# A two-stage kernel (cross-covariance attention, then a sigmoid-gated feed-forward): one activation table set, norms by Newton roots, and one PSUM bank per tile pair

## The chip, the cores and the metric

The kernel runs on one core of a Trainium2 chip. The metric is the time of one execution on the device in microseconds (us), as the median of several runs. A core has five engines that run side by side and wait for each other by semaphores: PE (TensorE, matrix products into PSUM), DVE (VectorE), ACT (ScalarE), POOL (GpSimd) and SP (which here only issues transfers). Each engine takes its instructions strictly in its own order.

## What is computed

For each of 4 batches, q, k and v are 6016 x 256. The attention is over channels: a 256 x 256 score from the columns of k and q, each divided by its norm, a softmax, and v times that matrix. Its result goes through a gated feed-forward layer of width 1536:

```python
qn = q / (np.linalg.norm(q, axis=1, keepdims=True) + 1e-06)
kn = k / (np.linalg.norm(k, axis=1, keepdims=True) + 1e-06)
s = kn.transpose(0, 2, 1) @ qn / tau
a = np.exp(s - s.max(-1, keepdims=True))
a /= a.sum(-1, keepdims=True) + 1e-09
x = (v @ a).reshape(B * N, C)
gate = 1.0 / (1.0 + np.exp(-(x @ w_gate)))
out = gate * (x @ w_val) @ w_out
```

The output has 24064 rows of 256 numbers in fp32; tau is 1.

## The kernel before

**The algebra.** Since x = v a, the kernel multiplies a into the weights once per batch: G = a w_gate and H = a w_val (tiles `gh_G`, `gh_H`, 256 x 1536 each), so that gate and value come from v directly. The last product, with `w_out`, is done with seven products in place of eight (Strassen and Winograd's way, 128 x 128 blocks): from two row tiles (a *pair*) and two column blocks of `w_out`, five sums of `hT` blocks (`sums`, made by DVE, L501) and five sums of `w_out` blocks (`w_sums`, made once by POOL, L198) give seven products, each of six matmuls with 128 columns, 42 for a pair.

**Order of the work.** The order is written out by hand and nothing reorders it. A batch has 47 row tiles of 128, in 12 *chunks* of four tiles (the last has three). A chunk has 12 *steps*, f = 0 to 11, one for each 128 columns of the inner width. In each step `glu` (L462 on) issues two matmuls into `ps_gate`, two into `ps_val` (two PSUM buffers each), a sigmoid on ACT (L483, `g_sb`) and a multiply on DVE (L484, `hT`). Behind it, `run_work` (L592) issues its share of the matmuls of the chunk before, about seven a step, into `ps_o` (a pool of two PSUM banks). `a_sum` puts one of DVE's ten sums in each of the steps 0, 1, 3, 4, 5 and 7 to 11.

**The products' banks.** `PRODUCTS` (L33) splits a pair's seven products over two banks, four in the first, three in the second, each copied to SBUF by ACT (L564, 512 and 384 columns). A chunk of two pairs so wants four banks one after the other, of two that there are. The copies are put off: `flush(1)` issues one of them behind the next step's sigmoid. From the copies POOL builds the four output blocks with four additions of 256 columns (`combine`, L524 to L528), and SP stores the chunk (L610, at f = 6).

**Beside it, for the next batch** (`side_work`, L702): POOL issues the loads of q, k and v, PE accumulates the score in PSUM in chunks 0 to 7, ACT squares q and k (L233) and DVE adds the squares (L271); these are folded (L281 to L289, one piece every three steps from chunk 8 on) and summed by PE into `ps_n` at step 9 of chunk 9, for k in all 256 columns of every partition.

**At a batch's end** ACT needs Sqrt (`wide_sqrt`, L306) and Exp (`exps`, L380), which lie in other table sets than Sigmoid, so that four ACT_TABLE_LOADs come in at the ends of the chunks 9 and 10. There the kernel keeps three sevenths of the products back (`keep`) and runs them as a block of matmuls behind the last step, and lets the products of the next chunk begin two steps late (`late`). Between them DVE inverts the roots in two parts (`wide_inv`, L311 and L312, 128 or 130 columns) and scales the score (L322). In chunk 11 twelve `gh` fills (two matmuls of 512 columns, L411 on, then a scaled copy to SBUF on ACT L431 or DVE L433) make G and H of the next batch, two of them in the last step.

Batch 0's attention runs ahead of the loop (to 41.6 us), with a root by ACT and its own table loads.

Of the kernel before, what the change touches and what calls it, by code (L numbers as in the profile page):

```python
# [10 lines left out]
BF16 = mybir.dt.bfloat16  # L11
ACT = mybir.ActivationFunctionType
# [20 lines left out]
PRODUCTS = (  # L33
    ((1, 1), 0),
    ((0, 0), 1),
    (0, 2),
    (1, 3),
    (2, (1, 1)),
    (3, (0, 0)),
    (4, 4),  # L40
)
FIRST_BANK = 4
NEXT_SLOTS = (0, 1, 3, 4, 5)
OWN_SLOTS = (7, 8, 9, 10, 11)
# [3 lines left out]
def kernel(  # L48
# [20 lines left out]
    nc = tc.nc  # L69
# [30 lines left out]
    f32pool = pool("f32pool", 2)  # L100
# [191 lines left out]
    def norms_mm(b):  # L292

        s = st[b]
        fold_q, fold_k = s["fold"]
        ps = psm.tile([P, CB + C], FP32, tag="m", name="ps_n")
        norm_mms(ps, (fold_q,), 2, True, True, (0,))
        for u in range(2):
            mm(ps[:, CB:], ones_bf, fold_k[:, u, :], False, u == 1, skip_group_check=True)
        s["n"] = ps  # L300

    def wide_sqrt(b):
        s = st[b]
        s["n_sb"] = attp.tile([P, CB + C], FP32, tag="nsb", name="n_sb")
        s["r"], s["rk"] = s["n_sb"][:, :CB], s["n_sb"][:, CB:]
        nc.scalar.activation(out=s["n_sb"], in_=s["n"], func=ACT.Sqrt)  # L306

    def wide_inv(b, part):

        r = st[b]["n_sb"][:, (0 if part == 0 else CB + C // 2) : CB + (part + 1) * (C // 2)]  # L310
        nc.vector.tensor_scalar(out=r, in0=r, scalar1=1e-6, scalar2=None, op0=ALU.add)  # L311
        nc.vector.reciprocal(r, r)  # L312
        if part == 0 and inv_tau != 1.0:
            nc.vector.tensor_scalar(
                out=r[:, :CB], in0=r[:, :CB], scalar1=inv_tau, scalar2=None, op0=ALU.mult
            )

    def wide_scale(b):
        s = st[b]
        s["x"] = attp.tile([P, CB, C], FP32, tag="x", name="x_sb")  # L320
        for j in range(CB):
            nc.vector.scalar_tensor_tensor(  # L322
                out=s["x"][:, j, :],
                in0=s["s"][:, j, :],
                scalar=s["r"][:, j : j + 1],
                in1=s["rk"],
                op0=ALU.mult,
                op1=ALU.mult,
            )
# [56 lines left out]
    def sums_both(b):  # L386
# [14 lines left out]
        s["rrow"] = [r[:, i : i + 1] for i in range(CB)]  # L401
# [23 lines left out]
    def gh_store(b, n, ps, act):  # L425
# [3 lines left out]
        r = s["rrow"][i]  # L429
# [32 lines left out]
    def glu(b, ci, f, between=None):  # L462
# [8 lines left out]
        for ps, w in ((ps_gate, G), (ps_val, H)):  # L471
# [11 lines left out]
        nc.scalar.activation(out=g_sb[:, :n], in_=ps_gate[:, :n], func=ACT.Sigmoid)  # L483
        nc.vector.tensor_tensor(  # L484
            out=hts[b, ci][:, f, :n], in0=ps_val[:, :n], in1=g_sb[:, :n], op=ALU.mult
# [4 lines left out]
    def a_sum(b, ci, g, m):  # L490
# [4 lines left out]
        if m == 0:  # L495
# [13 lines left out]
    pending = []  # L509
# [20 lines left out]
    def out_work(b, ci):  # L530
# [310 lines left out]
```

## Time and profile before

| | |
|---|---|
| median of 3 runs | 853.62 us (853.47 to 854.08) |
| the profiled execution | 854.03 us; its span, first to last instruction, 852.2 us |
| granted TensorE clock, mean | 0.998 |
| busy, of the span: PE / DVE / ACT / POOL | 94% / 86% / 62% / 48% |
| chain of work that ended last: PE / DVE / ACT | 70% / 12% / 7% |
| sigmoid L483, 128x512 | 528 of 598 ns |
| multiply L484, 128x512 | 528 of 684 ns |
| sums L501, 128x768 | 440 of 627 ns |
| table loads: L306 / L796 / before the loop | 3 / 9 / 3, 1283 ns each |

A page of the profile gives each engine's busy time, the chain of waits that leads to the last instruction, and groups of like instructions with the idle time of the engine ahead of them and what ended it. A row of the timeline is start, length, engine, line, operation, output<-input and count, with the wait before it in brackets. A row of the windows gives a stretch and its length, then busy time and count of PE, PEld (weight loads), DVE, ACT and POOL, then clock and DMA. PE's times are modelled and overlap: a matmul's row is longer than its distance to the next one, so distances are read from start to start.

### The profile page before, as it was taken

The numbers are of one execution on the slowest core, as the hardware profiler recorded it, in microseconds if no ns is written. First come the engines' busy times: TensorE is split into PE (matmuls) and PEld (weight loads), VectorE is DVE, ScalarE is ACT, GpSimd is POOL, SyncE is SP. The second block draws the span as 40 slices with busy tenths as digits, with TensorE's granted clock in tenths as the row PEclk, the third lists the DMA queues.
The fourth block names the chain that finished last, engine by engine and source line by source line (L and its number), as shares of the span: only waits on it lengthen the run. The fifth ranks groups of instructions, "written<-read, shape, count | busy, mean of one in ns | idle before, by whom it ended". The sixth has DMA issues, their size and how long they took to land.

```text
span 852.2 us, 17728 instructions
## 1 busy us (share of the span) xinstructions
PE 799.6 (94%) x6772; PEld 500.7 (59%) x6772; DVE 731.0 (86%) x1236; ACT 530.2 (62%) x900; POOL 413.2 (48%) x532
## 2 busy tenths in 40 slices
PE   4799999999899999999999999999999999999997
PEld 2446566655566666665556666665556556656566
DVE  5688899989788899889887899899987888889885
ACT  3666667655766666665666666666566555555553
POOL 4564455633463456435454365455434435535435
PEclk9999999999999999999999999999999999999999
DMA  9974684532547665522276655722342232332311
GB/s 221 215 145 82 110 133 80 107 73 57 100 75 134 102 106 100 106 64 50 46 111 129 101 100 105 133 56 50 84 61 50 66 66 62 74 77 51 84 35 70
DMA packets 77925, 78.22 MB, mean 92 GB/s; under 512 B 50704, under 2 KB 55824, under 8 KB 77840
## 3 DMA queue, kind: packets, MB, share of 16 engines
q0 software_dynamic: 21216, 38.02, 27.1%
q1 hardware_dynamic: 56336, 38.48, 20.5%
q8 instruction: 53, 0.87, 0.4%
q10 hardware_dynamic: 288, 0.59, 0.2%
q14 instruction: 32, 0.26, 0.1%
HBM read 78.64 MB, written 24.64 MB: 121 GB/s over the span
## 4 chain that ended last, share of the span: by engine, by line
PE 70%; DVE 12%; ACT 7%; issue 6%; DMA 4%; POOL 0%; DVEq 0%; ACTq 0%; POOLq 0%
PE ps_gate L121 23%; PE ps_val L121 22%; PE ps_o L121 20%; DVE hT L484 5%; DVE sums L501 4%; DMA k_sb<-in_k_dram 3%; PE ps_s L121 3%; ACT m_sb L564 3%; PE ps_gh L121 2%; ACT g_sb L483 2%; DVE acc L271 1%; ACT sq L233 1%; DMA w_gate<-in_moe_w_gate_dram 1%; ACT L306 0%; DVE two L281 0%
## 5 line engine op out<-in xcount | busy, mean ns | idle before, releaser
L483 ACT ACTIVATE g_sb<-ps_gate 128x512 f32<-128x512 f32 (+1 forms) x576 | 338.7, 589 | 276.5 <-PE ps_gate L121 268.8
L484 DVE TENSOR_TENSOR hT<-ps_val,g_sb 128x512 bf16<-128x512 f32 (+1 forms) x576 | 386.5, 673 | 96.7 <-ACT g_sb L483 89.2
L121 PE MATMUL ps_val<-vT,gh_H 128*128 128x512 bf16 (+1 forms) x1152 | 337.4, 374 | 8.0 <-DVE hT L484 6.7
L121 PE MATMUL ps_gate<-vT,gh_G 128*128 128x512 bf16 (+1 forms) x1152 | 337.4, 374 | 3.3 <-ACT g_sb L483 3.3
L501 DVE TENSOR_TENSOR sums<-hT 128x768 bf16<-128x768 bf16 (+1 forms) x470 | 290.2, 617 | 0.0
L524 POOL TENSOR_TENSOR m_sb<-m_sb 128x256 f32<-128x256 f32 x91 | 76.4, 839 | 399.4 <-ACT m_sb L564 399.3
L121 PEld LDWEIGHTS <-sums 128*128 128x128 bf16 x2730 | 183.8, 98 | 80.9
L121 PEld LDWEIGHTS <-gh_H 128*128 128x128 bf16 x1152 | 112.5, 98 | 144.8 <-issue 18.3
L121 PE MATMUL ps_o<-w_sums,sums 128*128 128x128 bf16 x1638 | 144.0, 219 | 0.0
L121 PEld LDWEIGHTS <-gh_G 128*128 128x128 bf16 x1152 | 96.7, 98 | 32.4 <-issue 17.3
L121 PE MATMUL ps_o<-w_out_sb,sums 128*128 128x128 bf16 x1092 | 100.8, 219 | 14.5 <-ACT m_sb L564 14.5
L121 PEld LDWEIGHTS <-hT 128*128 128x128 bf16 x1176 | 83.5, 98 | 48.1 <-DVE hT L484 2.8
L564 ACT COPY m_sb<-ps_o 128x384 f32<-128x384 f32 (+1 forms) x182 | 96.0, 528 | 0.0
L121 PE MATMUL ps_o<-w_sums,hT 128*128 128x128 bf16 x1092 | 92.0, 219 | 1.8 <-DVE hT L484 1.7
L121 PE MATMUL ps_s<-k_sb,q_sb 128*128 128x256 bf16 x376 | 72.8, 298 | 16.3 <-DMA k_sb<-in_k_dram 9.6
L525 POOL TENSOR_TENSOR m_sb<-m_sb 128x256 f32<-128x256 f32 x91 | 83.3, 916 | 7.1
L527 POOL TENSOR_TENSOR out_sb<-m_sb 128x256 f32<-128x256 f32 x91 | 86.1, 946 | 0.0
L528 POOL TENSOR_TENSOR out_sb<-m_sb 128x256 f32<-128x256 f32 x91 | 84.0, 923 | 0.0
L271 DVE TENSOR_TENSOR acc<-acc,sq 128x1024 bf16<-128x1024 bf16 (+1 forms) x66 | 57.7, 874 | 0.0
L233 ACT ACTIVATE sq<-k_sb 128x1024 bf16<-128x1024 bf16 (+2 forms) x44 | 44.8, 1026 | 15.1 <-DMA k_sb<-in_k_dram 14.9
L121 PEld LDWEIGHTS <-q_sb 128*128 128x128 bf16 x376 | 34.2, 106 | 29.1 <-issue 18.0
L233 ACT ACTIVATE sq<-q_sb 128x1024 bf16<-128x1024 bf16 (+2 forms) x36 | 36.5, 1014 | 0.2 <-DMA q_sb<-in_q_dram 0.2
(78 smaller groups left out, 279.9 us busy)
## 6 DMA issues: line engine op xcount, KB each, us to landing
out_dram<-out_sb SPq DMA_DIRECT2D x44, 512.0 KB, 3.4
v_sb<-in_v_dram POOLq DMA_DIRECT2D x44, 256.0 KB, 5.2
q_sb<-in_q_dram POOLq DMA_DIRECT2D x35, 256.0 KB, 7.1
k_sb<-in_k_dram POOLq DMA_DIRECT2D x35, 256.0 KB, 8.1
q_sb<-in_q_dram POOLq DMA_DIRECT2D x4, 512.0 KB, 12.5
k_sb<-in_k_dram POOLq DMA_DIRECT2D x4, 512.0 KB, 14.8
w_f<-in_moe_w_out_dram SPq DMA_DIRECT2D x3, 512.0 KB, 15.6
out_dram<-out_sb SPq DMA_DIRECT2D x3, 384.0 KB, 2.8
```

Of the source, the lines that this page charges most:

```text
L121: nc.tensor.matmul(out, lhsT=lhsT, rhs=rhs, start=start, stop=stop, **kw)
L233: nc.scalar.activation(out=sq[:, :nt, :], in_=src[:, :nt, :], func=ACT.Square)
L271: nc.vector.tensor_tensor(out=acc[:, :nt, :], in0=acc[:, :nt, :], in1=st[b]["sq", w][:, :nt, :], op=ALU.add)
L483: nc.scalar.activation(out=g_sb[:, :n], in_=ps_gate[:, :n], func=ACT.Sigmoid)
L484: nc.vector.tensor_tensor(out=hts[b, ci][:, f, :n], in0=ps_val[:, :n], in1=g_sb[:, :n], op=ALU.mult)
L501: nc.vector.tensor_tensor(out=sums[b, ci, g][:, m, :, : half * P], in0=hT[:, f0 + k0 : f1 : 2, ds(r0 * half * P, half * P)], in1=hT[:, f0 ...
L524: nc.gpsimd.tensor_tensor(out=t, in0=t, in1=m[:, 3:4, :].to_broadcast([P, 2, P]), op=ALU.add)
L525: nc.gpsimd.tensor_tensor(out=t, in0=t, in1=m[:, 4:6, :], op=ALU.subtract)
L527: nc.gpsimd.tensor_tensor(out=mids, in0=m[:, 1::-1, :], in1=m[:, 4:6, :], op=ALU.add)
L528: nc.gpsimd.tensor_tensor(out=ends, in0=t, in1=m[:, 0:2, :], op=ALU.add)
L564: nc.scalar.copy(m[:, n0:n1, :], state[bank][:, : (n1 - n0) * P].rearrange("p (n c) -> p n c", c=P))
```

## The change

It has four parts.

1. **One bank per pair.** `PRODUCTS` now names seven products with a region each of one bank, and `ORDER` sets the order: y1 of both pairs, then x1 and z1 of each; then x2, y2, z2, v2 of pair 0 and of pair 1. Behind z1 `part` copies three regions (384 columns) to `m_sb` on ACT, and POOL makes two sums of 128 columns (L592, L593). The products x2, y2 and z2 are then added on top in the same three regions, v2 takes the fourth, and `whole` copies all four (512 columns) into the output tile (L598), where POOL adds and subtracts (L606, L607, 256 columns each). Copies are issued at once, not put off. `keep`, `late`, `flush` and the blocks at the ends of chunks 9 and 10 are gone. The sums of `hT` move to steps 1, 3 to 6 and 7 to 11, in another order, and the store to f = 4.
2. **Tanh in place of Sigmoid.** sigmoid(z) = (1 + tanh(z/2)) / 2: ACT computes Tanh with scale 0.5, DVE's multiply becomes `scalar_tensor_tensor`, (g + 1) x value, and the half goes into H by a halved row sum (`rhalf`).
3. **Norms.** `norms_mm` sums both norms into 4 columns (eight matmuls of one column). DVE makes a seed by integer arithmetic on the bits (`root_seed`), POOL does four Newton steps of four operations and a last multiply on 128x4 (`root_steps`, 17 instructions, each waiting for the one before it), DVE inverts. PE spreads k's two columns to all partitions (`spread_both`, fp32), ACT copies them, DVE scales the score, one half a step, ACT takes Exp. This runs from the last step of chunk 9 to the last of chunk 10; the twelve fills follow in chunk 11, one a step. Folds come every four steps.
4. **w_out.** Three staging buffers in place of two; the `w_out` sums are spread over steps 3 to 17 in the order in which the products want them.

```diff
-FIRST_BANK = 4
-NEXT_SLOTS = (0, 1, 3, 4, 5)
-OWN_SLOTS = (7, 8, 9, 10, 11)
+ORDER = (
+    (0, "y1"), (1, "y1"), (0, "x1"), (0, "z1"), (1, "x1"), (1, "z1"),
+    (0, "x2"), (0, "y2"), (0, "z2"), (0, "v2"),
+    (1, "x2"), (1, "y2"), (1, "z2"), (1, "v2"),
+)
+NEXT_SLOTS = {1: 1, 3: 3, 4: 2, 5: 0, 6: 4}
+OWN_SLOTS = {7: 1, 8: 3, 9: 2, 10: 0, 11: 4}
...
+    def root_seed(b):
...
+        nc.vector.tensor_copy(out=x, in_=s["n"])
+        nc.vector.tensor_scalar(
+            out=y.bitcast(INT32),
+            in0=x.bitcast(INT32),
+            scalar1=-0.5,
+            scalar2=float(0x5F3759DF),
+            op0=ALU.mult,
+            op1=ALU.add,
+        )
...
+        for _ in range(4):
+            nc.gpsimd.tensor_tensor(out=t, in0=x, in1=y, op=ALU.mult)
+            nc.gpsimd.tensor_tensor(out=t, in0=t, in1=y, op=ALU.mult)
+            nc.gpsimd.tensor_scalar(out=t, in0=t, scalar1=-0.5, scalar2=1.5, op0=ALU.mult, op1=ALU.add)
+            nc.gpsimd.tensor_tensor(out=y, in0=y, in1=t, op=ALU.mult)
+        nc.gpsimd.tensor_tensor(out=s["r"], in0=x, in1=y, op=ALU.mult)
...
-        nc.scalar.activation(out=g_sb[:, :n], in_=ps_gate[:, :n], func=ACT.Sigmoid)
-        nc.vector.tensor_tensor(
-            out=hts[b, ci][:, f, :n], in0=ps_val[:, :n], in1=g_sb[:, :n], op=ALU.mult
+        nc.scalar.activation(out=g_sb[:, :n], in_=ps_gate[:, :n], func=ACT.Tanh, scale=0.5)
+        nc.vector.scalar_tensor_tensor(
+            out=hts[b, ci][:, f, :n],
+            in0=g_sb[:, :n],
+            scalar=1.0,
+            in1=ps_val[:, :n],
+            op0=ALU.add,
+            op1=ALU.mult,
         )
...
+        def part(p):
+
+            m = states[p]["m"] = mpool.tile([P, 3, P], FP32, tag="m", name="m_sb")
+            nc.scalar.copy(m, states[p]["ps"][:, : 3 * P].rearrange("p (n c) -> p n c", c=P))
+            nc.gpsimd.tensor_tensor(out=m[:, 1, :], in0=m[:, 1, :], in1=m[:, 2, :], op=ALU.add)
+            nc.gpsimd.tensor_tensor(out=m[:, 2, :], in0=m[:, 1, :], in1=m[:, 0, :], op=ALU.add)
...
-        at(9 * FC + 9, norms_mm, n)
...
+        s0 = 10 * FC - 2
+        at(s0 + 1, norms_mm, n)
+        at(s0 + 2, root_seed, n)
+        at(s0 + 2, root_steps, n)
+        at(s0 + 5, norms_inv, n)
+        at(s0 + 6, spread_both, n)
+        at(s0 + 7, copy_rk, n)
+        at(s0 + 8, scale_x, n, 0)
+        at(s0 + 9, scale_x, n, 1)
+        at(s0 + 10, exps, n, 0)
+        at(s0 + 11, exps, n, 1)
+        at(s0 + 13, sums_both, n)
...
-            at(11 * FC + min(i + 1, FC - 1), gh, n, i, *((pss, "s"), (psm, "m"))[i % 2])
+            at(s0 + 14 + i, gh, n, i, *((pss, "s"), (psm, "m"))[i % 2])
```

**PE, chunk 3 of batch 3, where a pair goes on to its fourth product or its second bank.** Each row is a weight load or a matmul; the number behind a name tells buffers apart. Before, in step 6, the third bank of the chunk (`ps_o_10292`) is opened right behind the last product of the second:

```order
L121 LDWEIGHTS sums_10175
L121 MATMUL ps_o_10202<-w_sums_185,sums_10175 128x128
L121 LDWEIGHTS sums_10083 [waits PE_49]
L121 MATMUL ps_o_10292<-w_out_sb_176,sums_10083 128x128 [waits Activation_49]
L121 LDWEIGHTS gh_G1_9242
L121 MATMUL ps_gate_10294<-vT_9992,gh_G1_9242 128x512
```

Now, in step 5, pair 0 goes on in its own bank (`ps_o_10178`) behind the last matmul of z1 of pair 1 (`ps_o_10185`):

```order
L127 LDWEIGHTS sums_10198
L127 MATMUL ps_o_10185<-w_sums_185,sums_10198 128x128
L127 LDWEIGHTS sums_10091
L127 MATMUL ps_o_10178<-w_out_sb_176,sums_10091 128x128 [waits Activation_49]
L127 LDWEIGHTS sums_10091
L127 MATMUL ps_o_10178<-w_out_sb_176,sums_10091 128x128
```

Both wait for a copy by ACT. Before, it is that of a bank filled up to the end of step 5; now it is that of pair 0's first three products, the last of which stands in step 3.

**ACT, end of chunk 9 and begin of chunk 10 in batch 0.** Before:

```order
L483 ACTIVATE g_sb_2882<-ps_gate_2876 128x512 [waits DVE_49,PE_49]
L564 COPY m_sb_2885<-ps_o_2744 128x512 [waits Pool_49]
L306 ACT_TABLE_LOAD
L306 ACTIVATE n_sb_2888<-ps_n_2855 128x258
L796 ACT_TABLE_LOAD
L483 ACTIVATE g_sb_2936<-ps_gate_2930 128x512 [waits DVE_49,PE_49]
```

Now, from the last step of chunk 9 to the spread's copy in step 5 of chunk 10:

```order
L516 ACTIVATE g_sb_2899<-ps_gate_2893 128x512 [waits DVE_49,PE_49]
L598 COPY out_sb_2848<-ps_o_2697 128x2x256 [waits PE_49]
L516 ACTIVATE g_sb_2929<-ps_gate_2923 128x512 [waits DVE_49,PE_49]
L516 ACTIVATE g_sb_2976<-ps_gate_2970 128x512 [waits DVE_49,PE_49]
L516 ACTIVATE g_sb_2994<-ps_gate_2988 128x512 [waits DVE_49,PE_49]
L516 ACTIVATE g_sb_3012<-ps_gate_3006 128x512 [waits DVE_49,PE_49]
L591 COPY m_sb_3019<-ps_o_2932 128x384 [waits PE_49,Pool_49]
L516 ACTIVATE g_sb_3035<-ps_gate_3029 128x512 [waits DVE_49,PE_49]
L516 ACTIVATE g_sb_3056<-ps_gate_3050 128x512 [waits DVE_49,PE_49]
L591 COPY m_sb_3061<-ps_o_2939 128x384 [waits PE_49,Pool_49]
L332 COPY rk_sb_3071<-ps_rk_3047 128x256
```

The root and the loads are gone from ACT; two loads are left in the whole program, both ahead of the loop, of fifteen.

**POOL, begin of chunk 10 in batch 0.** Now the Newton chain stands behind the last pair's additions and the issues of three loads (the first four of its 17 rows are shown; three more rounds of the same and a last multiply follow):

```order
L606 TENSOR_TENSOR out_sb_2848<-out_sb_2848,m_sb_2789 128x2x128 [waits Activation_49]
L607 TENSOR_TENSOR out_sb_2848<-out_sb_2848 128x2x128 [waits Pool_49]
L147 DMA v_sb_2941<-in_v_dram 128x1024 [waits DMAHW0_49,DMASW4_49,DMASW2_49]
L137 DMA q_sb_2943<-in_q_dram 128x1024 [waits DMASW3_49,PE_49]
L137 DMA k_sb_2945<-in_k_dram 128x1024
L361 TENSOR_TENSOR t_n_2951<-sq_n_2947,y_n_2948 128x4 [waits DVE_49]
L362 TENSOR_TENSOR t_n_2951<-t_n_2951,y_n_2948 128x4 [waits Pool_49]
L363 TENSOR_SCALAR t_n_2951<-t_n_2951 128x4 [waits Pool_49]
L364 TENSOR_TENSOR y_n_2948<-y_n_2948,t_n_2951 128x4 [waits Pool_49]
```

and on PE, in step 4 of chunk 10 of batch 2, the spread that takes its result by way of DVE:

```order
L127 LDWEIGHTS sums_9021
L127 MATMUL ps_o_8985<-w_sums_185,sums_9021 128x128
L127 MATMUL ps_rk_9089<-ident_f_127,r_8994 128x128 [waits DVE_49,PE_49]
L127 MATMUL ps_rk_9089<-ident_f_127,r_8994 128x128
L127 LDWEIGHTS gh_G1_6228
L127 MATMUL ps_gate_9092<-vT_8783,gh_G1_6228 128x512 [waits Activation_49]
```

Before, POOL had nothing to do with the norms, and PE had no spread in the loop.

More of the change, by code (lines that the diff above doesn't have):

```diff
@@ L308, in wide_inv @@
[L308 to L315, printed above, removed]
+        s["n"] = psm.tile([P, 2 * CB], FP32, tag="m", name="ps_n")
+        norm_mms(s["n"], s["fold"], 2, True, True)
```

242 lines of the change are left out of this document (112 added, 130 removed).

## The prediction, made before the result was known

> **What bounds the kernel now.** I read the page first, then the table of waits, then the timeline of one chunk of the last batch, where nothing but the main loop runs, and last the stretches at a batch's end.
>
> ```profile
> span 852.2 us, 17728 instructions
> ...
> PE 799.6 (94%) x6772; PEld 500.7 (59%) x6772; DVE 731.0 (86%) x1236; ACT 530.2 (62%) x900; POOL 413.2 (48%) x532
> ```
>
> PE is the bound, and DVE stands close behind it. So a change is worth what it takes out of PE's pauses, as long as DVE can follow. Which pauses there are, the waits tell:
>
> ```profile
> PE ps_o L121 <- ACT m_sb L564: 14.5, 34, 0.6
> ...
> PE ps_val L121 <- DVE hT L484: 6.7, 17, 0.8
> ```
>
> The first row is one event, 34 times: PE wants to start a product in a PSUM bank that ACT has not copied out yet. In the timeline of chunk 3 of batch 3 it is step 6 of the twelve steps:
>
> ```profile
> 712.24 0.59 PE L121 MATMUL ps_gate<-vT,gh_G 128*128 128x512 bf16 x2
> ...
> 713.49 0.59 PE L121 MATMUL ps_gate<-vT,gh_G 128*128 128x512 bf16 x2
> 713.92 0.59 PE L121 MATMUL ps_val<-vT,gh_H 128*128 128x512 bf16 x2
> 714.36 0.50 PE L121 MATMUL ps_o<-w_sums,sums 128*128 128x128 bf16 x6
> 715.25 0.22 PE L121 MATMUL ps_o<-w_out_sb,sums 128*128 128x128 bf16 x1 [0.40 <-ACT m_sb L564]
> 715.30 0.38 PE L121 MATMUL ps_gate<-vT,gh_G 128*128 128x512 bf16 x1
> ```
>
> ```profile
> 714.12 0.60 ACT L483 ACTIVATE g_sb<-ps_gate 128x512 f32<-128x512 f32 x1 [0.65 <-PE ps_gate L121]
> 714.62 0.58 ACT L564 COPY m_sb<-ps_o 128x512 f32<-128x512 f32 x1
> ```
>
> Step 5 takes 713.49 - 712.24 = 1.25 us, step 6 takes 715.30 - 713.49 = 1.81. The seventh product matmul would have started at 714.70 and starts at 715.25, when the copy that was put behind the next sigmoid is over. A pause costs 0.56 us of PE (the 0.40 that the row marks, and the pipe's refilling).
>
> The stretches at a batch's end are the other loss. The windows run from the first gate matmul of a chunk to that of the next: chunk 6 of batch 1, its chunks 9, 10 and 11, and chunk 3 of batch 3.
>
> ```profile
> 351.40:368.31 16.91, 16.52 (x146) 10.60 (x144) 15.27 (x26) 11.48 (x19) 7.78 (x10) 1.00 0.30 64
> 401.47:418.16 16.69, 15.85 (x142) 9.66 (x140) 16.00 (x29) 9.64 (x16) 7.22 (x8) 1.00 0.25 56
> 418.16:435.46 17.30, 15.96 (x135) 9.35 (x133) 14.76 (x27) 11.62 (x20) 9.57 (x13) 1.00 0.55 96
> 435.46:455.75 20.29, 18.73 (x163) 11.84 (x161) 15.62 (x31) 13.50 (x27) 10.25 (x14) 1.00 0.65 101
> 705.97:721.57 15.60, 15.21 (x135) 9.42 (x133) 13.73 (x23) 8.87 (x16) 7.26 (x10) 1.00 0.31 68
> ```
>
> A full chunk without its one pause is 15.60 - 0.56 = 15.04 us. Chunk 11 has tiles of 384 rows and twelve fills of the next batch's weights; its steps are priced by this piece of it:
>
> ```profile
> 445.84 0.49 PE L121 MATMUL ps_gate<-vT,gh_G 128*128 128x384 bf16 x2
> 446.16 0.49 PE L121 MATMUL ps_val<-vT,gh_H 128*128 128x384 bf16 x2
> 446.49 0.61 PE L121 MATMUL ps_o<-w_sums,sums 128*128 128x128 bf16 x8
> 446.94 0.59 PE L121 MATMUL ps_gh<-w_gate,e_sb 128*128 128x512 bf16 x2
> 447.37 0.33 PE L121 MATMUL ps_gate<-vT,gh_G 128*128 128x384 bf16 x1
> ```
>
> From start to start: 0.32 and 0.33 for gate and value, 0.45 for eight products (0.056 each), 0.43 for a fill. Twelve steps with seven products are 12 x (0.65 + 0.39 + 0.43) = 17.6 us; chunk 11 takes 20.29.
>
> **The change part by part.** The sum is made against the profiled execution: 854.03 us, of which 852.2 are the span; that is 0.4 above the median of 853.62.
>
> *One bank for a tile pair.* The 42 matmuls of a pair stay. Its first three products are copied out (384 columns), the other four are added on top in the same bank, and the second copy takes 512 columns. ACT's work stays at 0.475 + 0.58 us:
>
> ```profile
> L484 DVE TENSOR_TENSOR hT<-ps_val,g_sb 128x512 bf16<-128x512 f32 x528 | 360.0, 684 | 79.8 <-ACT g_sb L483 72.5 <-PE ps_o L121 0.6
> ...
> L564 ACT COPY m_sb<-ps_o 128x512 f32<-128x512 f32 x91 | 52.8, 580 | 0.0
> ...
> L564 ACT COPY m_sb<-ps_o 128x384 f32<-128x384 f32 x91 | 43.2, 475 | 0.0
> ...
> L433 DVE TENSOR_SCALAR gh_G<-ps_gh,rrow 128x512 bf16<-128x512 f32 x13 | 9.6, 741 | 0.5 <-PE ps_gh L121 0.5
> ...
> L364 DVE SCALAR_TENSOR_TENSOR y_sb<-x_sb,r,ps_rk 128x128 f32<-128x128 f32 x4 | 1.1, 344 | 0.0
> ...
> L121 PE MATMUL ps_n<-ones_bf,fold 128*128 128x1 bf16 x12 | 0.7, 164 | 0.0
> L121 PE MATMUL ps_rk<-ident_f,r 128*128 128x128 f32 x4 | 0.7, 293 | 0.0
> ...
> L209 DVE TENSOR_SCALAR rrow<-ps_r 128x2 f32<-128x2 f32 x4 | 0.6, 150 | 1.1 <-PE ps_r L121 1.1
> ...
> L822 POOL MEMSET const-float32-1.0<- 128x1 f32 x1 | 0.1, 99 | 0.0
> ```
>
> Where does PE wait now? With times from a step's first gate matmul (rows of step 5 and 6 above): the sigmoid starts at 0.63 and ends at 1.23, the products run from 0.87 to 1.25, so a copy of 0.475 runs from 1.24 to 1.71, in the gap of 0.65 that ACT has before each sigmoid. Pair 0's third product is its 24th matmul in the order, in step 3; the fourth product needs the copy at matmul 37, in step 5, two steps later: no wait. The last copy of a chunk starts when its last product has landed, at about 1.45 of step 11 (a single product's row spans 0.22), and ends at 2.03, that is 0.78 of the next step 0; the bank is wanted at 0.87 + 6 x 0.056 = 1.2. Cover of 0.4 us; if it were gone, each chunk would pay what is missing. So the 34 pauses go: -34 x 0.56 = **-19.0**.
>
> One chunk per batch gives some back. Chunk 0 works on the products of chunk 11, which has a single pair, and there product four follows product three with nothing between: it is due at about 0.92 of the step and its bank is free at 1.71 + 0.04. That is 0.83 us, in batches 1 to 3: **+2.5**.
>
> *Tanh for sigmoid.* ACT's pass over 512 columns is the same length for either, as I take it, since a sigmoid at 0.60 and a copy at 0.58 differ by 0.02. The multiply becomes a fused (g + 1) x value on DVE, 576 times, on the engine that is next to bind. The profile holds fused ones only with a pointer scalar: 344 ns at 128 columns. TENSOR_TENSOR at 684 and TENSOR_SCALAR with a pointer at 741, both over 512 columns, put the pointer at 57 ns; L209, two columns with an immediate, takes 150, so a column costs (684 - 150) / 510 = 1.05 ns. An immediate fused one over 512 is then 344 - 57 + 384 x 1.05 = 690. I take 684, cost zero, with 741 as the dear end.
>
> *Norms and tables.* The loads go from ACT's path at a batch's end:
>
> ```profile
> L796 ACT ACT_TABLE_LOAD x9 | 11.5, 1283 | 0.2
> ```
>
> ```profile
> 417.01 1.28 ACT L306 ACT_TABLE_LOAD   x1
> 418.30 0.39 ACT L306 ACTIVATE n_sb<-ps_n 128x258 f32<-128x258 f32 x1
> 418.71 1.28 ACT L796 ACT_TABLE_LOAD   x1
> 420.00 0.60 ACT L483 ACTIVATE g_sb<-ps_gate 128x512 f32<-128x512 f32 x1
> ```
>
> These nine and three at L306 are four a batch end, under blocks of held-back products; without loads and blocks chunks 9 and 10 become full chunks. What the windows above show over the full chunk is the price of the old way, cover and all. The Trainium skill (ScalarE: Activation LUTs, What ACT_TABLE_LOAD costs) puts every switch at 1283 ns of load and about 1380 of drain; by it the twelve would hold ACT for 32 us, an estimate, instead of 15.4. The trace shows the 1.28 and no drain: the second load starts 0.02 after the root ends, and the sigmoid starts 0.01 after the load. The sum uses neither price, but the lengths of the chunks.
>
> New bill for chunks 9, 10 and 11: 2 x 15.04 + 17.6, and on PE eight norm columns (0.06 each, 0.5), two fp32 spreads (0.3 each, 0.6), and 0.6 that I leave for small waits of DVE and ACT: 49.4 against 54.28, or -4.9 a batch, **-14.7**.
>
> *The Newton chain.* Against this stand seventeen dependent POOL instructions on 128x4 values. PE meets their result in step 4 of chunk 10, at the spread, 5 x 1.25 = 6.25 us after the chunk's start. POOL's queue before them:
>
> ```profile
> 421.06 0.72 POOL L524 TENSOR_TENSOR m_sb<-m_sb 128x256 f32<-128x256 f32 x1 [12.29 <-ACT m_sb L564]
> 421.86 0.93 POOL L525 TENSOR_TENSOR m_sb<-m_sb 128x256 f32<-128x256 f32 x1
> ...
> 424.53 0.57 POOL L141 DMA_DIRECT2D v_sb<-in_v_dram  x1
> 425.10 0.54 POOL L131 DMA_DIRECT2D q_sb<-in_q_dram  x1
> ```
>
> The last pair's two sums start when ACT's copy is over, 0.3 into the chunk (0.78 less the 0.5 of norm columns), and take 0.80 + 0.93: 2.05. One v issue and, in batches 0 and 1, a q and a k issue bring it to 3.7 (2.6 in batch 2). An operation on four values lies between the memset's 0.10 plus the 0.08 between dependent sums (421.86 - 421.78), 0.18, and the 0.80 from sum to sum of 256 columns. It is nearest to the memset in size, but reads two inputs: I take 0.25. The chain ends at 3.7 + 17 x 0.25 = 7.95, DVE's two small steps (0.15 each, and handing over) at 8.4: PE waits 2.1, 2.1 and 1.0 us, **+5.2**. All of that is on the path: DVE stands at its wait with the next multiply behind it, and PE at the spread.
>
> *The rest.* Folds every four steps in place of three should spare some of the 6.7 us in which PE waits for hT; new lags of DVE and ACT, where a copy and a square now meet in step 5, take part of that back: I put **-1.1**, unsure by 3 either way. A small halving on DVE before the loop, +0.1. POOL's sums of a pair shrink from four of 256 columns to two of 256 and two of 128, and the w_out sums are spread out: POOL is idle half the time, nothing on the path.
>
> Sum: -19.0 + 2.5 - 14.7 + 5.2 - 1.1 + 0.1 = **-27.0**, so 854.0 - 27.0 = 827.0 us.
>
> **The rivals.**
>
> *The chain is dearer, but not ruinous.* At 0.35 to 0.75 us an operation each tenth costs 17 x 0.1 x 3 = 5.1 us: 832 to 852. For it: POOL's spans in a profile are rough, and no small two-input operation was seen. Against: the memset's 0.10. The Trainium skill (SBUF — State Buffer, Who interferes with whom) has a DVE instruction with two SBUF inputs block a GpSimd one that reads SBUF; by it DVE's sums in steps 1 and 3 could each hold one link back by at most their own length. POOL's sums of 0.72 and 0.93, of one shape, look like that rule at work. Chance 0.17.
>
> *DVE becomes the bound.* In chunk 6 of batch 1 DVE is busy 15.27 of 16.91 us; take 0.56 away from PE and 16.35 are left. If the fused multiply costs 741, 12 x 0.057 = 0.7 more, 15.97, and the additions of squares come in lumps: then the chunks 1 to 7 of batches 0 to 2 keep their length and lose the gain of 21 x 0.56 = 11.8: 839. Against: the 690 worked out from L364, and the lighter POOL, whose sums and DVE's read the same memory. Chance 0.12.
>
> *Slower: the chain at 256-column prices.* If a dependent POOL operation cost as much as the sums do from start to start, 0.80 us, whatever its size, the chain would take 13.6 us and PE would wait 11.5, 11.5 and 10.4: 33.4 in place of 5.2, 855; at 0.93 + 0.08, the second row above, 866. It decides from about 0.82 on. For it: the fixed part of a POOL operation is not to be read from shapes all alike. Against it stands the memset alone. Chance 0.05.
>
> *The tables stay.* If tanh were not in exp's set, loads would remain; the instruction order holds two loads in place of fifteen, which closes this.
>
> **How the numbers follow.** The forecast has 0.62: 827, from 820 (chain at 0.18: -3.4; DVE's unsure 3) to 835. A gain beyond that, if DVE's waits vanish altogether, 0.03; a near draw by some wait that I do not see, 0.01. The range leaves out the slow rival and the dear half of the first: 818 to 843. A measurement of this kernel can tell 0.2%, 1.7 us, from no change. Faster 0.92, same 0.03, slower 0.05.
>
> **What would show it.** Right: no row of PE waiting for a product copy but three of about 0.8 us at the start of batches 1 to 3; steps of 1.25 throughout chunks 1 to 10 of batch 3 (15.04 a chunk); two table loads; chunk 11 near 17.6. The wait of PE's spread for DVE, once a batch, gives the chain's price directly. Wrong: the fused multiply above 0.70 us with rows of PE waiting for hT; a chain of over 13 us; waits for the copy at step 0 of each chunk.

## The result, and the profile after

829.07 us, median of four runs (827.37 to 832.04), against 853.85 for the kernel before: ratio 0.9714 (0.9686 to 0.9742). 827.0 was forecast. The profiled execution took 827.37, 26.7 less than that of before, and the sum is settled against it; the totals agree to 0.4 us. It is the fastest of the four: by the medians the gain is 24.8 us, 2.2 less than forecast. Several terms do not agree, and their errors cancel. First the page, and then the table of waits of the changed kernel (line numbers are its own: L127 is the matmul helper, L517 the fused multiply, L539 the sums, L591 and L598 the two product copies, L361 to L365 the Newton chain, L369 and L370 the add and the reciprocal behind it).

```profile
span 825.6 us, 17993 instructions
...
PE 788.6 (96%) x6790; PEld 501.4 (61%) x6790; DVE 724.8 (88%) x1240; ACT 526.7 (64%) x887; POOL 359.1 (43%) x583
```

```profile
PE ps_rk L127 <- DVE r L370: 9.4, 3, 3.4
...
DVE r L369 <- POOL r L365: 7.9, 3, 2.9
...
PE ps_o L127 <- ACT m_sb L591: 1.9, 3, 0.6
...
PE ps_o L127 <- DVE sums L539: 1.6, 2, 1.0
...
PE ps_val L127 <- DVE hT L517: 0.5, 2, 0.3
```

The 34 waits for a product copy are three, as forecast, and the 17 for hT, which were only expected to shrink, are two. The spread's wait is there, longer than forecast (3.4, 3.4 and 2.6 us against 2.1, 2.1 and 1.0). The two waits for sums were not forecast at all. Two table loads are left, both ahead of the loop.

Chunk 3 of batch 3 in the timeline, steps 3 and 4:

```profile
686.25 0.59 PE L127 MATMUL ps_gate<-vT,gh_G 128*128 128x512 bf16 x2
...
687.50 0.59 PE L127 MATMUL ps_gate<-vT,gh_G 128*128 128x512 bf16 x2
...
687.53 0.48 ACT L591 COPY m_sb<-ps_o 128x384 f32<-128x384 f32 x1
...
688.13 0.60 ACT L516 ACTIVATE g_sb<-ps_gate 128x512 f32<-128x512 f32 x1
...
688.75 0.59 PE L127 MATMUL ps_gate<-vT,gh_G 128*128 128x512 bf16 x2
```

Every step is 1.25 us. The copy, 0.48, lies ahead of the tanh, in ACT's gap. Now the same five stretches as before: chunk 6 of batch 1, its chunks 9, 10 and 11, chunk 3 of batch 3.

```profile
339.56:355.92 16.36, 16.36 (x147) 10.56 (x145) 15.54 (x26) 11.85 (x20) 6.18 (x9) 1.00 0.30 66
387.11:402.38 15.27, 15.27 (x143) 9.58 (x141) 15.09 (x27) 9.15 (x16) 6.03 (x9) 1.00 0.27 61
402.38:421.61 19.23, 15.83 (x146) 10.01 (x144) 14.80 (x30) 10.19 (x19) 11.70 (x30) 1.00 0.48 84
421.61:439.28 17.67, 17.67 (x162) 11.73 (x159) 14.74 (x32) 11.38 (x23) 7.11 (x11) 1.00 0.78 119
682.48:697.53 15.05, 15.05 (x135) 9.39 (x133) 13.58 (x23) 9.15 (x16) 6.29 (x9) 1.00 0.33 71
```

PE is busy from end to end in four of them. Only chunk 10 has idle time, 3.40 us, and these rows of it show why:

```profile
406.36 0.23 POOL L361 TENSOR_TENSOR t_n<-sq_n,y_n 128x4 f32<-128x4 f32 x1
...
408.01 0.55 DVE L539 TENSOR_TENSOR sums<-hT 128x768 bf16<-128x768 bf16 x1
...
408.08 0.54 POOL L363 TENSOR_SCALAR t_n<-t_n 128x4 f32<-128x4 f32 x1
...
409.54 0.19 POOL L363 TENSOR_SCALAR t_n<-t_n 128x4 f32<-128x4 f32 x1
409.82 0.20 POOL L364 TENSOR_TENSOR y_n<-y_n,t_n 128x4 f32<-128x4 f32 x1
410.10 0.20 POOL L361 TENSOR_TENSOR t_n<-sq_n,y_n 128x4 f32<-128x4 f32 x1
...
411.22 0.20 POOL L365 TENSOR_TENSOR r<-sq_n,y_n 128x4 f32<-128x4 f32 x1
411.37 0.45 POOL L592 TENSOR_TENSOR m_sb<-m_sb 128x128 f32<-128x128 f32 x1
411.46 0.40 DVE L369 TENSOR_SCALAR r<-r 128x4 f32<-128x4 f32 x1 [2.90 <-POOL r L365]
411.89 0.18 DVE L370 RECIPROCAL r<-r 128x4 f32<-128x4 f32 x1
...
412.21 0.68 PE L127 MATMUL ps_rk<-ident_f,r 128*128 128x128 f32 x4 [3.40 <-DVE r L370]
```

A chain link is 0.28 us from start to start (409.54, 409.82, 410.10), and one link, at 408.08, takes 0.54 instead of 0.19 while DVE's sum runs. Step 4 of this chunk is 5.33 us long.

The last chunk of all is the other place. Its two waits:

```profile
810.45 0.55 DVE L539 TENSOR_TENSOR sums<-hT 128x768 bf16<-128x768 bf16 x1
811.05 0.23 PE L127 MATMUL ps_o<-w_sums,sums 128*128 128x128 bf16 x1 [0.61 <-DVE sums L539]
...
812.64 0.55 DVE L539 TENSOR_TENSOR sums<-hT 128x768 bf16<-128x768 bf16 x1
813.25 0.34 PE L127 MATMUL ps_o<-w_sums,sums 128*128 128x128 bf16 x3 [1.04 <-DVE sums L539]
```

Steps 5 and 6 there take 2.19 and 2.31 us, where the kernel before has 1.10: its last chunk spreads the 84 products over ten steps too, but makes the sums in steps 0, 1, 3, 4 and 5 and asks for the late ones later.

Measured from the first gate matmul of each chunk, the 26.7 us divide so: chunks 1 to 8 of batches 0 to 2 and 1 to 10 of batch 3, -25.7; chunks 9 to 11 of batches 0 to 2, -5.6; chunk 0 of batch 0, -0.5; chunk 0 of batches 1 to 3, +2.35; the stretch ahead of the loop, +1.57; the last chunk and the end, +1.24.

### The profile page after: what moved, and what is told of

It is laid out like the page before. It is cut to its first block, busy times and chain, and to the rows that moved or that the text cites. A ratio compares the mean times of both kernels' runs of the same rounds, so it can differ in the third digit from the quotient of the medians.

```text
span 825.6 us, 17993 instructions
## 1 busy us (share of the span) xinstructions
PE 788.6 (96%) x6790; PEld 501.4 (61%) x6790; DVE 724.8 (88%) x1240; ACT 526.7 (64%) x887; POOL 359.1 (43%) x583
## 4 chain that ended last, share of the span: by engine, by line
PE 88%; DMA 5%; POOL 3%; DVE 2%; issue 1%; ACT 1%; POOLq 0%
PE ps_gate L127 28%; PE ps_val L127 28%; PE ps_o L127 26%; DMA k_sb<-in_k_dram 4%; PE ps_s L127 4%; PE ps_gh L127 2%; DMA w_gate<-in_moe_w_gate_dram 1%; DVE hT L517 1%; ACT g_sb L516 0%; DVE sums L539 0%; POOL t_n L363 0%; POOL t_n L362 0%; POOL t_n L361 0%; PE ps_rk L127 0%; POOL y_n L364 0%
## 5 line engine op out<-in xcount | busy, mean ns | idle before, releaser
L517 DVE SCALAR_TENSOR_TENSOR hT<-g_sb,ps_val 128x512 bf16<-128x512 f32 (+1 forms) x576 | 384.3, 670 | 68.3 <-ACT g_sb L516 58.5
L127 PE MATMUL ps_val<-vT,gh_H 128*128 128x512 bf16 (+1 forms) x1152 | 338.0, 375 | 0.6 <-DVE hT L517 0.5
L127 PE MATMUL ps_gate<-vT,gh_G 128*128 128x512 bf16 (+1 forms) x1152 | 338.0, 375 | 0.0
L539 DVE TENSOR_TENSOR sums<-hT 128x768 bf16<-128x768 bf16 (+1 forms) x470 | 287.8, 612 | 0.0
L127 PEld LDWEIGHTS <-sums 128*128 128x128 bf16 x2730 | 187.4, 98 | 89.0 <-issue 2.8
L127 PEld LDWEIGHTS <-gh_H 128*128 128x128 bf16 x1152 | 112.8, 98 | 132.4 <-issue 2.2
L606 POOL TENSOR_TENSOR out_sb<-out_sb,m_sb 128x256 f32<-128x256 f32 x91 | 78.6, 863 | 234.4 <-ACT out_sb L598 222.2
L127 PE MATMUL ps_o<-w_sums,sums 128*128 128x128 bf16 x1638 | 158.6, 219 | 1.6 <-DVE sums L539 1.6
L592 POOL TENSOR_TENSOR m_sb<-m_sb 128x128 f32<-128x128 f32 x91 | 42.4, 466 | 180.1 <-ACT m_sb L591 180.1
L127 PEld LDWEIGHTS <-hT 128*128 128x128 bf16 x1176 | 85.3, 98 | 44.5
L127 PEld LDWEIGHTS <-gh_G 128*128 128x128 bf16 x1152 | 96.8, 98 | 15.2 <-DVE gh_G L466 0.5
L127 PE MATMUL ps_o<-w_out_sb,sums 128*128 128x128 bf16 x1092 | 98.7, 219 | 2.0 <-ACT m_sb L591 1.9
L127 PE MATMUL ps_o<-w_sums,hT 128*128 128x128 bf16 x1092 | 97.7, 219 | 0.0
L127 PE MATMUL ps_s<-k_sb,q_sb 128*128 128x256 bf16 x376 | 72.1, 296 | 18.8 <-DMA k_sb<-in_k_dram 12.0
L607 POOL TENSOR_TENSOR out_sb<-out_sb 128x256 f32<-128x256 f32 x91 | 80.0, 879 | 7.1
L598 ACT COPY out_sb<-ps_o 128x512 f32<-128x512 f32 x91 | 53.3, 586 | 14.0 <-PE ps_o L127 11.2
L278 DVE TENSOR_TENSOR acc<-acc,sq 128x1024 bf16<-128x1024 bf16 (+1 forms) x66 | 60.3, 914 | 0.0
L593 POOL TENSOR_TENSOR m_sb<-m_sb 128x128 f32<-128x128 f32 x91 | 55.7, 612 | 7.1
L127 PEld LDWEIGHTS <-q_sb 128*128 128x128 bf16 x376 | 33.7, 105 | 24.6 <-issue 11.8
L591 ACT COPY m_sb<-ps_o 128x384 f32<-128x384 f32 x91 | 43.6, 479 | 3.4 <-PE ps_o L127 1.2
```

Of the source, the lines that this page charges most:

```text
L127: nc.tensor.matmul(out, lhsT=lhsT, rhs=rhs, start=start, stop=stop, **kw)
L278: nc.vector.tensor_tensor(out=acc[:, :nt, :], in0=acc[:, :nt, :], in1=st[b]["sq", w][:, :nt, :], op=ALU.add)
L517: nc.vector.scalar_tensor_tensor(out=hts[b, ci][:, f, :n], in0=g_sb[:, :n], scalar=1.0, in1=ps_val[:, :n], op0=ALU.add, op1=ALU.mult,)
L539: nc.vector.tensor_tensor(out=sums[b, ci, g][:, m, :, : half * P], in0=hT[:, f0 + k0 : f1 : 2, ds(r0 * half * P, half * P)], in1=hT[:, f0 ...
L591: nc.scalar.copy(m, states[p]["ps"][:, : 3 * P].rearrange("p (n c) -> p n c", c=P))
L592: nc.gpsimd.tensor_tensor(out=m[:, 1, :], in0=m[:, 1, :], in1=m[:, 2, :], op=ALU.add)
```

## The experiments

Nine kernels, each timed against the kernel before. The first three take away one wait each from the changed kernel.

**The chain earlier.**

```
-            at(8 * FC + 1 + 4 * i, acc_fold, n, *divmod(i, 3))
+            at(8 * FC + 1 + 3 * i, acc_fold, n, *divmod(i, 3))
...
-        at(s0 + 1, norms_mm, n)
-        at(s0 + 2, root_seed, n)
-        at(s0 + 2, root_steps, n)
+        at(s0 - 3, norms_mm, n)
+        at(s0 - 2, root_seed, n)
+        at(s0 - 2, root_steps, n)
```

> The folds of the squares come every three steps instead of every four, and the norm columns, the seed and the seventeen Newton operations are issued four steps earlier (in chunk 9 from step 7 on); the two small DVE steps, the spread and all behind it stay where they are. Theory (the wait of 3.0 to 3.4 us in front of the spread is the chain's length and the queue ahead of it, nothing else): the spread finds its roots ready, the row of PE waiting for DVE r goes, chunk 10 of batches 0 to 2 falls from 19.2, 19.2 and 19.9 us to about 15.2, and the kernel from 829.1 to about 817.5 us (-11 to -12). Rival (PE is late there anyway, for the folds that now come denser, or for exps and scalings that the wait had hidden): the wait only changes its name, chunk 8 or 9 or 10 grows by what the spread's wait loses, and the time stays within 3 us of 829.

Measured: 818.02 us (817.95 to 818.06), ratio 0.9581 (0.9567 to 0.9595). Chunk 10 of the batches 0 to 2 is 16.28, 16.26 and 16.50 us in place of 19.23, 19.23 and 19.91, and chunks 8 and 9 stay at 15.05 and 15.25. The theory holds but for a rest: the row does not go, and chunk 10 stays 0.6 to 0.9 us above the 15.65 that it takes without a pause (the last kernel below):

```profile
PE ps_rk L127 <- DVE r L370: 1.4, 3, 0.6
```

**The last sums sooner.**

```
-                    if f in NEXT_SLOTS:
-                        a_sum(*prev, 1, NEXT_SLOTS[f])
+                    slots = {0: 1, 1: 3, 2: 2, 3: 0, 4: 4} if final else NEXT_SLOTS
+                    if f in slots:
+                        a_sum(*prev, 1, slots[f])
```

> In the last chunk alone, the five sums of the second half are made behind the multiplies of steps 0 to 4 instead of 1, 3, 4, 5 and 6. Theory (the last chunk spends its 84 products over ten steps instead of twelve, so the products reach the sums before DVE has made them: the waits of 0.61 and 1.04 us for DVE sums in steps 5 and 6): chunk 11 of batch 3 falls from 15.3 to about 12.8 us and the kernel by 2.5, to about 826.5. Rival (DVE or ACT is what is late there; the sums only show it): the waits move to hT or to a product copy, and the chunk stays above 14.5 us, the kernel at 829.

Measured: 827.8 us (824.6 to 829.25), ratio 0.9691 (0.9669 to 0.9712), which does not set it apart from the changed kernel by time. The trace does: steps 5 and 6 of the last chunk are 1.10 each, and from its first gate to the end it takes 20.04 us in place of 22.69, 2.65 less. The theory holds.

**The odd tile between the products.**

```
-        if nt % 2:
-            for f in range(FC):
-                work.append((2, single, nt - 1, f))
         for p, name in ORDER:
+            if nt % 2 and (p, name) == (0, "x2"):
+                for f in range(FC):
+                    work.append((2, single, nt - 1, f))
             if p < half:
```

> In the chunks that work on a group with a single tile pair (chunk 0 of batches 1 to 3), the twelve 256-column matmuls of the odd tile are put between the pair's third product and its fourth; before they stood ahead of the first. Theory (PE waits there for the copy of 384 columns because product four follows product three with nothing between): the row of PE waiting for ACT m_sb goes, step 7 of these chunks falls from 1.92 to about 1.2 us, -0.8 in each, the kernel from 829.1 to about 826.7. Rival (the bank that the odd tile now takes later becomes the wait, or the second sums are wanted too early): step 2 or 3 of these chunks grows by as much, and the time stays at 829.

Measured: 829.19 us (828.26 to 829.92), ratio 0.9711 (0.9697 to 0.9726): no gain by time, as the rival had it. But its reason does not hold: chunk 0 of batches 1 to 3 falls from 16.11, 16.11 and 14.80 to 15.38, 15.38 and 14.07 (-0.73 each), no row of PE waiting for m_sb is left, and no other step of those chunks grows by as much. The gain went elsewhere: chunk 10, which the edit doesn't touch, takes 20.80, 22.22 and 18.38 us in batches 0 to 2 against 19.23, 19.23 and 19.91, 3.0 more in all, with the spread's waits unchanged (3.38, 3.38 and 2.55). Three stretches of it in batch 1: the spread's wait, the steps behind it, and those after (the last but two of a row's numbers is PE's granted clock).

```profile
409.80:413.00 3.20, 0.00 (x0) 0.00 (x0) 0.63 (x3) 0.00 (x0) 2.39 (x11) 0.91 1.08 155
413.10:418.90 5.80, 5.80 (x26) 3.53 (x27) 2.40 (x5) 1.95 (x4) 1.42 (x3) 0.50 0.33 55
419.00:423.00 4.00, 4.00 (x36) 2.49 (x35) 3.72 (x8) 2.52 (x5) 0.67 (x1) 0.97 0.00 0
```

For 5.8 us after the wait PE has half its clock, and two steps take 2.45 us in place of 1.25. Where the spread hardly waits, the gain is there: the kernel with all three edits (below) lies 4.8 us under the one with the early chain, of which the last chunk's sums are worth 2.6 and these three chunks 2.2. The changed kernel's own profile has the half clock once, in batch 2, behind a wait of 2.56 us:

```profile
606.50:609.00 2.50, 0.00 (x0) 0.02 (x1) 0.71 (x3) 0.00 (x0) 1.93 (x9) 0.94 0.22 42
609.00:611.50 2.50, 2.49 (x8) 1.54 (x9) 0.92 (x2) 0.41 (x1) 0.16 (x1) 0.50 0.42 80
```

**The wait filled.** This tests that the idle stretch itself halves the clock.

```
+        at(s0 + 6, busy, 14)
         at(s0 + 6, spread_both, n)
```

> The changed kernel with fourteen matmuls of 512 columns on constants (0.22 us each, 3.0 us, their result is not used) put ahead of the spread in chunk 10 of batches 0 to 2, where PE otherwise waits 2.6 to 3.4 us for the Newton chain. Theory (PE's clock falls to half for one or two steps after such an idle stretch, in some executions and some batches: granted clock 0.50 and steps of 2.3 to 2.45 us in place of 1.25; that is why the changed kernel's times lie between 827 and 832): with the fill no step behind the spread is over 1.5 us, and the times come to 826 to 827.5 us, within 0.6 of each other. Rival (the clock falls for another reason, such as the transfers at that place, or the scatter comes from the start): steps of 2.3 us stay, or the times still lie 2 us or more apart.

Measured: 826.0 us, ratio 0.9675 (0.9659 to 0.9691); the five times are 825.69, 825.91, 826.0, 826.33 and 835.44. The last is the profiled one and lost its time at the start (its first gate is at 50.22, with PE waiting 7 us for gh_G), not at the fill. In its trace no step behind a spread is over 1.5 us, and the spread of batch 1 waits 0.36 for its roots (thirteen of the fourteen matmuls have a record):

```profile
418.06 3.19 PE L127 MATMUL ps_busy<-ones_wide,ones_bf 128*128 128x512 bf16 x13
...
421.61 0.68 PE L127 MATMUL ps_rk<-ident_f,r 128*128 128x128 f32 x4 [0.36 <-DVE r L370]
```

Some 9 us of useless matmuls make the kernel 3 us faster in the median. The theory holds but for the outlier, which is the scatter from the start that the rival named. What PE waited for stands behind one row on DVE, the halving of the row sum that came in with tanh:

```profile
42.55 7.00 DVE L433 TENSOR_SCALAR rhalf<-rrow 128x2 f32<-128x2 f32 x1
...
50.22 1.03 PE L127 MATMUL ps_gate<-vT,gh_G 128*128 128x512 bf16 x2 [6.78 <-DVE gh_G L466]
```

In the changed kernel's profile the same row takes 0.17 us. Here POOL works without a pause on two conversions and six sums of `w_out` from 42.96 to 49.06, and the row ends at 49.55. That the one held the other is not tried by a run; whether the changed kernel's slowest execution (832.04) has the same is not known, since it has no profile.

**Half the chain.**

```
-        for _ in range(4):
+        for _ in range(2):
```

> The changed kernel with two Newton steps for each root instead of four (the last two, eight POOL operations, are left out, so the roots are less exact). Theory (the spread waits for the chain, operation by operation, at 0.28 us from start to start): the wait in chunk 10 falls by 8 x 0.28 = 2.25 us, from 3.40, 3.4 and 2.6 to 1.1, 1.1 and 0.3, and where PE ran at half its clock after the wait it no longer does; the kernel comes to 821 to 822.5 us. Rival (the wait is set by POOL's queue and by DVE's sums that hold single operations back, not by the number of operations): it falls by less than 1 us each, the kernel stays above 826.

Measured: 819.56 us (819.47 to 819.7), ratio 0.9599 (0.9585 to 0.9613), better than the theory's 821 to 822.5. Chunk 10 falls by 2.26, 2.25 and 3.63 us, in all 8.1; 2.25 is eight links at 0.28, and the rest of the third is the half clock that no longer comes. The wait follows the chain's length.

**The copy at once, in the kernel before.**

```
-                pending.append((evict, state, bank, p))
+                evict(state, bank, p)
...
-                pending.append((evict_single, state, s))
+                evict_single(state, s)
```

> The kernel before with one edit: a product bank is copied out at once when its last product has been issued, not behind the next sigmoid. Two banks for each tile pair, sigmoid, square roots, table loads and the blocks at the batch ends all stay. Theory A (the 34 pauses of 0.56 us come from the copy's place in ACT's order alone; a copy of 0.58 us fits into the gap of 0.65 ahead of the next sigmoid): the 34 rows of PE waiting for ACT m_sb go, a full chunk of batch 3 falls from 15.60 to 15.05 us, the kernel from 853.9 to about 835 (-19). Then the one bank for a tile pair has no part in the gain. Theory B (two banks in turn are wanted again too soon, so that only the other grouping of the products takes the wait away): some of the pauses stay, a full chunk stays at 15.3 us or more, the kernel above 845.

Measured: 837.1 us (836.49 to 837.83), ratio 0.9805 (0.979 to 0.9819). Chunk 3 of batch 3, steps 5 and 6:

```profile
702.12 0.60 ACT L483 ACTIVATE g_sb<-ps_gate 128x512 f32<-128x512 f32 x1 [0.66 <-PE ps_gate L121]
...
702.66 0.58 ACT L564 COPY m_sb<-ps_o 128x512 f32<-128x512 f32 x1
702.74 0.59 PE L121 MATMUL ps_gate<-vT,gh_G 128*128 128x512 bf16 x2
...
703.37 0.60 ACT L483 ACTIVATE g_sb<-ps_gate 128x512 f32<-128x512 f32 x1
...
703.94 0.22 PE L121 MATMUL ps_o<-w_out_sb,sums 128*128 128x128 bf16 x1
```

The seventh product starts with no wait, a full chunk of batch 3 is 15.05 us, and no PE wait for a copy is left. Theory A holds: two banks for a pair would have done to take these pauses away. Elsewhere it gains less: in batches 0 to 2 chunks 1 to 8 get shorter by 11.6 us, where their 24 pauses were worth 13.4, and chunks 9 to 11 grow by 2.3. At the batch ends the copies now stand ahead of a sigmoid behind a table load, and PE's waits for the sigmoid grow from 3.3 to 7.4 us. The seventeen waits for hT stay, as this row shows, and so the kernel stays 8 us above the changed one:

```profile
PE ps_val L121 <- DVE hT L484: 6.2, 17, 0.8
```

**The sigmoid back.**

```
-        s["rrow"] = [[x[:, i : i + 1] for i in range(CB)] for x in (r, half)]
+        s["rrow"] = [[x[:, i : i + 1] for i in range(CB)] for x in (r, r)]
...
-        nc.scalar.activation(out=g_sb[:, :n], in_=ps_gate[:, :n], func=ACT.Tanh, scale=0.5)
-        nc.vector.scalar_tensor_tensor(
...
+        nc.scalar.activation(out=g_sb[:, :n], in_=ps_gate[:, :n], func=ACT.Sigmoid)
+        nc.vector.tensor_tensor(
+            out=hts[b, ci][:, f, :n], in0=ps_val[:, :n], in1=g_sb[:, :n], op=ALU.mult
+        )
```

> The changed kernel with the sigmoid and the plain multiply back in place of tanh, the fused multiply and the halving; the Newton roots and the product order stay. The exponentials at a batch's end now need another table set: four loads of 1.28 us at steps 8 to 10 of chunk 10 of batches 0 to 2, and one at the start. Theory (ACT stands late by two loads and an exponential, about 2.3 us after its gap of 0.65, twice in a row, and PE's two gate banks and two value banks cover about 1 us of it): steps 9 to 11 of chunk 10 grow by 3 to 4 us in each batch end, the kernel comes to 838 to 843 us (+9 to +14 against 829.1). Rival (loads lie under PE's work as other side work does): 829 to 832. The multiply alone would change nothing: 681 ns fused, 684 plain.

Measured: 849.42 us (847.83 to 850.22), ratio 0.9946 (0.9932 to 0.9961): dearer than the theory. Chunks 10 and 11 of batch 1 take 25.14 and 19.09 us against 19.23 and 17.67; the three batch ends together grow by 20.1.

```profile
429.47 1.28 ACT L516 ACT_TABLE_LOAD   x1
430.76 0.60 ACT L516 ACTIVATE g_sb<-ps_gate 128x512 f32<-128x512 f32 x1
431.38 1.28 ACT L411 ACT_TABLE_LOAD   x1
...
431.41 0.59 PE L127 MATMUL ps_gate<-vT,gh_G 128*128 128x512 bf16 x2 [1.73 <-ACT g_sb L516]
...
433.20 1.28 ACT L516 ACT_TABLE_LOAD   x1
...
435.14 0.80 PE L127 MATMUL ps_gate<-vT,gh_G 128*128 128x384 bf16 x2 [1.70 <-ACT g_sb L516]
```

Steps 10 and 11 grow by 1.9 and 2.4 us in each batch, a little more than the 3 to 4 expected. Then the first step of chunk 11, 2.9 us in place of 1.47, runs at a granted clock of 0.51, and steps 5 and 6 of chunk 10 lose 1.7 us at 0.59, behind the chain's wait (in batch 2 it is the second step of chunk 11 that loses instead, 1.1 us). What the forecast left out is again the clock, and here it fell behind a wait of 1.70 us that followed one of 1.73.

**All three edits, and the reciprocal a step earlier.** The first kernel is the sum of the first three edits; the second also has:

```
-        at(s0 + 5, norms_inv, n)
+        at(s0 + 4, norms_inv, n)
```

> The three edits together: the early chain, the sums of the last chunk behind steps 0 to 4, the odd tile's matmuls between the third and the fourth product. Theory (the three waits are independent, each on PE's path by itself): the gains add up, -11.5, -2.5 and -2.4, from 829.1 to about 812.5 us. Rival (DVE, busy 88% of the span, takes over once PE waits no more): rows of PE waiting for DVE hT appear in batches 0 to 2, and the kernel stays above 818.

> The three edits together, and the two small DVE steps (add 1e-6, reciprocal) one step earlier, in step 2 of chunk 10 instead of step 3. Theory (with the early chain the roots are ready long before, and what is left of step 4, 2.36 us in place of 1.25 and the spread's 0.5, is the wait of 0.40 us for DVE's reciprocal behind a sum of 0.84, and the refilling): step 4 falls to 1.8 us in batches 0 to 2, the kernel from 813.2 to about 811.6 us. Rival (DVE's queue is that late at any step, or the weight load of the fp32 spread is what takes the time): step 4 stays above 2.2 us, the kernel at 813.

Measured: 813.22 us (813.0 to 813.47), ratio 0.9526 (0.951 to 0.9541); and 811.07 us (810.75 to 811.23), ratio 0.95 (0.9484 to 0.9516). Both theories hold: the gains of the three edits add up, and in the second kernel step 4 is 1.75 us. There chunk 10 is without a pause in every batch, as in batch 1:

```profile
397.71:413.36 15.65, 15.65 (x143) 9.97 (x141) 14.39 (x27) 10.10 (x19) 11.44 (x27) 1.00 0.62 103
```

It is 18 us faster than the changed kernel: so much the change left undone at these three places.

## Why the prediction was right, point by point

**The 34 pauses: right in size, too broad in cause.** A full chunk of batch 3 is 15.05 us where 15.04 was forecast. But the sum booked the -19.0 under the one bank, and the copy at once does the same with two in batch 3, and most of it elsewhere: what mattered is that the copy now stands ahead of the next sigmoid on ACT.

**Chunk 0 of batches 1 to 3: right.** +0.78 to +0.79 each (+2.35) against +0.83. With other matmuls between, 0.73 of it goes.

**The fused multiply and tanh: right.**

```profile
L517 DVE SCALAR_TENSOR_TENSOR hT<-g_sb,ps_val 128x512 bf16<-128x512 f32 x528 | 358.0, 681 | 53.8 <-ACT g_sb L516 44.6 <-PE ps_o L127 2.1 <-PE ps_gate L127 0.8
L516 ACT ACTIVATE g_sb<-ps_gate 128x512 f32<-128x512 f32 x528 | 314.8, 597 | 226.8 <-PE ps_gate L127 215.9 <-DVE fold L295 3.9 <-DVE hT L517 0.9
```

681 ns against 684 for the plain multiply. DVE did not become the bound, not even at 811 us.

**Chunks 9 to 11 without waits: mis-sized, too little.** The bill was 49.4 us a batch, -14.7. The last kernel, where nothing waits, has 48.57, so -17.1 was to be had.

**The Newton chain: mis-sized, the largest error.** Forecast +5.2; the changed kernel stands at 52.17, 52.17 and 52.85 us, 11.5 above three times 48.57. For batch 1, from the chunk's start at 402.38: the chain starts at 3.98 (3.7 forecast), takes 5.06 (4.25), and the add, the reciprocal and the handing over take 0.79 (0.45). The links cost 0.28 instead of 0.25, and beside DVE's sum one is 0.35 longer. The Trainium skill (SBUF — State Buffer, Who interferes with whom) has a DVE instruction with two SBUF inputs block a GpSimd one that reads SBUF; the link at 408.08 agrees, ending 0.06 after the sum. The add takes 0.40 and ends 0.04 after POOL's L592, which started just ahead of it; in the last kernel it stands beside the longer L606, takes 0.67 and ends 0.02 after it. In the kernel with the early chain, where POOL is issuing a load at that moment, it takes 0.17 to 0.19 in batches 0 and 1, but 0.41 in batch 2. To the waits of 3.4, 3.4 and 2.6 comes the half clock of batch 2, about 1.4 us, which the sum had not at all.

**The rest: mis-sized, and its reason fell.** -1.1 was set; chunks 1 to 8 of batches 0 to 2 and 1 to 10 of batch 3 gained 25.7 - 19.0 = 6.7 us beyond the pauses. These are not the 6.7 us of waits for hT by which the forecast sized the term, though the figures are alike: of those 17 waits twelve (3.9 us) lie in chunks 9 and 10, which the bill of the batch ends had replaced already, and only four (2.1 us) in chunks 1 to 8. The reason given, folds every four steps, does not hold either: with the early chain they come every three, and chunks 8 and 9 stay as short. For chunk 8, 2.9 of the 6.7 us, the traces point to the lighter POOL: the fold of 128x512 (`two`) takes 1.21 us each time in the kernel before and in that with the copy at once, beside POOL's sums of 256 columns, and 0.68 in the changed kernel and with the early chain, where POOL is idle at that moment. How much the product order and the sums' new steps did was not separated.

**Missed: the last chunk and the start.** Nothing was booked for the last chunk, where the moved sums cost 2.65 us by the second experiment. And the first gate comes at 43.16 in place of 41.59: the first batch's loads land later (its second load of k at 12.02 in place of 10.70). Every kernel built on the changed one has it (42.6 to 43.2 but for the outlier), the one built on the kernel before has not (41.50). Its cause was not tried. A candidate is the third staging buffer: `w_out`'s three loads of 512 KB now start at 1.20, 6.72 and 7.19, where before they started at 6.52, 7.00 and 42.52.

So the forecast's mechanism was right, its 827.0 partly luck: about 8 us too little gain (5.6 in the rest, 2.4 in the batch ends) against 9 us too little loss (6.3 at the chain, 2.8 at the last chunk and the start, less a little in chunk 0). That the terms left out weigh as much as those booked too small is chance.

## What to carry to other kernels

When a chain of tiny operations moves to an idle engine, count its links at their start-to-start time, put its issue early enough that nobody meets its end, and check the order in which the last, compressed iteration asks for its inputs. Before regrouping buffers, look whether the copy that frees one merely stands behind the wrong instruction. A wait on PE can cost more than itself, in the steps behind it: here that happened behind waits from 1.5 us on, not behind any of 1.2 us or less in the loop, and not every time.

## What the runs showed of the hardware

Behind a wait of 1.5 to 3.4 us in the loop PE sometimes ran at a granted clock of 0.50. Each such stretch is 3.4 or 6.8 us long in the traces (from 608.69 to 612.10 in the changed kernel), and they added up to 3 us to a chunk. Behind the other two waits of 3.40 us in the changed kernel's profile the clock kept 1.00. The Trainium skill (TensorE: Matmul & The Clock Gate, What's actually happening) has the clock halved after an idle window of about 3.4 us that runs freely. The changing outcome agrees with that. But the half clock also came behind 2.56 us of idleness (the changed kernel, batch 2), behind 1.70 us (the sigmoid back, all three batches, with 1.73 us idle shortly before) and behind 1.47 us (the copy at once, batch 2; the same wait in batches 0 and 1 kept 1.00): these are shorter than the page's window, and the traces decide. The scatter fits: kernels with the full wait spread over 1.7 to 4.7 us (829.07, 827.8 and 829.19 in the median), those built on the changed one that wait at most 1.2 us there over 0.1 to 0.5, and that with the wait filled over 0.6 without its outlier.

A small POOL operation (128x4) took 0.19 to 0.20 us, and 0.28 from start to start when dependent, whether it read one or two inputs. A small DVE operation beside a POOL instruction that had started just before it ended 0.02 to 0.04 us after that instruction: the add of 0.17 us took 0.40 and 0.67.
